# A transformer block's forward and backward: one DMA transpose of the attention backward is held back until the next block's double transpose and issued directly ahead of it

## The chip, the core and the metric

The kernel runs as one program on one core of a Trainium2 chip. The core has five engines that this document names as the profile does: PE (TensorE, matrix products and transposes into PSUM), DVE (VectorE), ACT (ScalarE), POOL (GpSimd) and SP (SyncE). SP computes nothing here: its instruction queue issues nearly all DMA transfers, one after the other. The metric is the device time of one execution in microseconds (us), compared as the median over several executions.

## The reference, cut to what matters

The program returns the output of a parallel block and the gradients of its input and of five weight matrices. `x` is 2048 tokens by 448 features, there are 16 heads of 28 features, and the feed-forward part has 1792 hidden units.

```
xn  = layernorm(x)
qkv = xn @ wqkv                               # 16 heads, Dh = 28
p   = softmax(q @ k.T * Dh**-0.5)             # per head, 2048 x 2048
out = x + (p @ v) @ wo + (silu(xn @ w_gate) * (xn @ w_up)) @ w_down
_, vjp = jax.vjp(f, x, wqkv, wo, w_gate, w_up, w_down)
grads  = vjp(grad_out)                        # six gradients
```

What the change touches is the attention backward: per head, `ds = p * (dO @ v.T - delta)` is formed tile by tile, and the gradient of the queries is `dq = ds @ k * scale`. Here `ds` has query rows on the partitions, and the product for `dq` needs it with key rows on the partitions, so every `ds` tile is transposed once. The gradients of `k` and `v` take `ds` and `p` as they are.

## The kernel before, in words

**Forward, to about 617 us.** The projections, the attention forward, the feed-forward part and its weight gradients are interleaved by hand. Queries, keys and what the backward needs of them (tensors `QD_d` and `KD_d`) are written to device memory.

**Backward, from about 617 us.** A list `steps` of 512 steps runs over 4 groups of heads (`g`), 2 pairs of heads in each (`hp`), 4 key chunks of 512 (`kc`), 4 query chunks (`qc`) and 4 query tiles of 128 (`qi`). Four steps with the same `qc` make a **block**; there are 128 blocks, numbered `b` from 0. One step treats one query tile against 512 keys for two heads (`j` = 0, 1). The main loop (L1235) goes through `k`, and iteration `k` does, in program order:

- `row(k)` (L802): two score products into PSUM tiles `sb` for step `k` (L810), and two products into PSUM tiles `db` for step `k-1` (L818).
- `ew(k)` (L833): two exponentials on ACT for step `k` (tile `e_sb`, L837) and two multiplications on DVE for step `k-1`, which write the tile `ds_sb` (L845). One `ds_sb` tile holds two query tiles: `qi` 0 and 1, or `qi` 2 and 3. There are five such buffers. After the multiplications of `qi` 1 and of `qi` 2 it calls `dst_dma`.
- stores that have come due (`flush`, L797, issued from L800) and loads that are spread over the steps (`drop`, L755, issued from L767); all go to the SP queue. The loads fill query and key tiles (`qd`, `kd`), and the operands of other products that are slipped in between the steps (`h_c`, `x_c`, `o_c`, `dau_c`, `wguT`, `dc`).
- `kv` (L907): four products for the gradients of keys and values (L918, L922).
- once per block, `tr_unit(b)` at `k = 4b + 8`: the `ds` tile of `qi` 3 is transposed on PE (L900) and copied to `dsT` by ACT (L905). In the last block `qi` 2 goes this way as well.
- once per block, `dq_unit(b)` at `k = 4b + 13`: 16 products (L949) of the block's `dsT`, then one addition into `dq_acc`.
- pieces of other products in the time that is left (`fill_step`).

**The transposes by DMA.** `dst_dma(b, ds, qi)` (L824) is called twice per block. At `qi` 1 it takes a new `dsT` buffer (three of them) and issues one DMA transpose of two query tiles from SP; this document calls it the **double** (L830, 128 times). At `qi` 2 it issues one of one query tile, the **third** (L826, 127 times, since the last block has none). With block `b` the double is issued in iteration `4b + 2`, the third in `4b + 3`.

**Who waits for them.** `dq_unit(b)` on PE needs both. The DVE multiplication that takes the same `ds_sb` buffer again, five tiles later, needs the transpose to have read it: for the double that is in iteration `4b + 11` (block `b + 2`, `qi` 2), for the third in `4b + 13` (block `b + 3`, `qi` 0).

**What sets the order.** Every engine runs its instructions in program order and waits by semaphores where data or buffers are missing. SP is such an engine: a transfer stands behind all that were given to SP before it, whether its own data are there or not. Each DMA of SP also waits for the one eight places earlier, since eight semaphores are used in turn.

Of the kernel before, what the change touches and what calls it, by code (L numbers as in the profile page):

```python
# [103 lines left out]
def kernel(  # L104
# [23 lines left out]
    PE, DVE, ACTE, POOL, SP = nc.tensor, nc.vector, nc.scalar, nc.gpsimd, nc.sync  # L128
# [418 lines left out]
    for i in range(len(chain) + LEAD):  # L547
# [4 lines left out]
        k = i - LEAD  # L552
        if k >= 0:
            b = chain[k]
# [98 lines left out]
    for t in range(4):  # L653
        run(T_unit(xnT, xn_t, t, t % 2 == 0, ps_s if t < 2 else None))
    DVE.tensor_reduce(out=r_ones[:],
                      in_=ident_f[:].rearrange("p (a b) -> p a b", b=HP)[:, :, 28:30],
# [11 lines left out]
    for c in range(3):  # L668
        k = 4 * c
# [116 lines left out]
    dqT, dkv, acc, dsT = {}, {}, {}, {}  # L786
# [34 lines left out]

    bk, pend = None, []

    def dst_dma(b, ds, qi):  # L824
        if qi == 2:
            SP.dma_start_transpose(out=dsT[b][:, 2].rearrange("p j kt s -> p (j kt) s"),  # L826
                                   in_=ds[:, 0].rearrange("p j k -> p (j k)"))
            return
        dsT[b] = bk.tile([P, 4, 2, 4, P], BF16, name="dsT", bufs=3)
        SP.dma_start_transpose(out=dsT[b][:, 0:2].rearrange("p q j kt s -> p (q j kt) s"),  # L830
                               in_=ds[:].rearrange("p q j k -> p (q j k)"))

    def ew(k):  # L833
        if k < NB:
            est[k] = kq.tile([P, 2, 512], BF16, name="e_sb", bufs=5)
            for j in range(2):
                ACTE.activation(out=est[k][:, j], in_=sps.pop((k, j))[:], func=ACT.Exp, scale=SCALE)  # L837
        if 1 <= k <= NB:
            g, hp, kc, qc, qi = steps[k - 1]
            b = (k - 1) // 4  # L840
            if qi % 2 == 0:
                dss[k - 1] = dss[k] = kq.tile([P, 2, 2, 512], BF16, name="ds_sb", bufs=5)
            ds = dss[k - 1]
            for j in range(2):
                DVE.tensor_tensor(out=ds[:, qi % 2, j], in0=dps.pop((k - 1, j))[:], in1=est[k - 1][:, j], op=ALU.mult)  # L845
            if qi == 1 or qi == 2 and b < NB // 4 - 1:
                if bk is None:
                    pend.append(lambda: dst_dma(b, ds, qi))
                else:
                    dst_dma(b, ds, qi)  # L850
# [9 lines left out]
    k = n = 0  # L860
# [374 lines left out]
    for k in range(NB + 12):  # L1235
# [21 lines left out]
        if m == 0:  # L1257
            b = (k - 8) // 4
# [6 lines left out]
        elif m == 1:  # L1265
            b = (k - 13) // 4
# [122 lines left out]
```

The softmax here doesn't subtract the row's maximum and nothing guards it: scores larger than these inputs give would overflow.

## Time and profile before

| What | Value |
|---|---|
| median of 13 runs | 1467.3 us (1464.23 to 1475.64) |
| the profiled execution, its time | 1468.93 us |
| the profiled execution, its span | 1467.1 us |
| granted TensorE clock, mean | 0.977 |
| PE, DVE, ACT busy | 92%, 79%, 86% of the span |
| queue of the transfers that SP issues (q1) | 86.9% of 16 DMA engines' span |
| doubles, L830 | 128, median 3067 ns on the SP queue |
| thirds, L826 | 127, median 1256 ns on the SP queue |

The profile is one execution, recorded by the hardware. Its span is the time from the first instruction to the last. A page of it lists groups of instructions by line; in a row like `L845 DVE TENSOR_TENSOR ds_sb<-db,e_sb ... x1024 | 648.6, 685 | 68.8 <-PE db L818 21.8` the line is followed by the engine, the operation, the tile written and the tiles read, the number of instructions, the busy time and the mean of one in ns, and then the engine's idle time directly before these instructions with what ended most of it. `SPq` rows are DMA instructions on the SP queue; their duration is how long the queue was held by the issue, and the data land later. A list of waits names who waited for whom, with the sum, the number of times and the longest. A timeline gives rows in order of time: start, duration, engine, line, operation, tiles, count, and in brackets the idle time before.

### The profile page before, as it was taken

To read this page: it belongs to the slowest core of one execution; us is meant where nothing else is said; L and a number is where in the kernel's file an instruction comes from. 1 tells how busy PE (TensorE), PEld (TensorE's weight loads), DVE (VectorE), ACT (ScalarE), POOL (GpSimd) and SP (SyncE) were. 2 spreads that over 40 slices of the span, in tenths; PEclk is the share of its full clock that TensorE was granted. 3 is DMA by queue.
4 is the path that set the end of the run, shared out by engine and by line. 5 is a ranking of instruction groups with operands and counts; after the bars stand their busy time and mean duration, and the time that the engine had idled before them with its cause. 6 is when DMAs were issued, how large, how long until landed. Compare 5 with 4: busy or idle time off the path is not lost. (4 is left out here: it accounts for less than half of the span.)

```text
span 1467.1 us, 34402 instructions
## 1 busy us (share of the span) xinstructions
PE 1345.0 (92%) x12708; PEld 543.4 (37%) x12708; DVE 1154.5 (79%) x1997; ACT 1262.6 (86%) x2193; POOL 362.6 (25%) x486
## 2 busy tenths in 40 slices
PE   5899999989999999898999989999899999899996
PEld 2333333333333333332333334433343444343343
DVE  6577756756667667487898879888889999899988
ACT  5798989988999988687798979899889999888974
POOL 6465514553344444010001101001001011010005
PEclk9899999999999999998999999999999999999998
DMA  5797957696678675799999999999999999999971
GB/s 151 160 205 184 219 116 187 156 198 163 156 173 186 141 183 132 207 191 198 215 202 202 214 207 188 204 200 209 218 198 189 206 211 214 214 190 196 206 143 59
DMA packets 697664, 271.14 MB, mean 185 GB/s; under 512 B 616128, under 2 KB 672152, under 8 KB 697496
## 3 DMA queue, kind: packets, MB, share of 16 engines
q1 hardware_dynamic: 692520, 262.82, 86.9%
q0 software_dynamic: 3568, 5.83, 1.9%
q8 instruction: 100, 1.64, 0.5%
q14 instruction: 68, 0.56, 0.1%
q10 hardware_dynamic: 1408, 0.30, 0.1%
HBM read 65.04 MB, written 59.90 MB: 85 GB/s over the span
## 5 line engine op out<-in xcount | busy, mean ns | idle before, releaser
L845 DVE TENSOR_TENSOR ds_sb<-db,e_sb 128x512 bf16<-128x512 f32 x1024 | 648.6, 685 | 68.8 <-PE db L818 21.8
L837 ACT ACTIVATE e_sb<-sb 128x512 bf16<-128x512 f32 x1024 | 554.8, 611 | 63.2 <-PE db L818 47.0
L611 ACT ACTIVATE eT<-s_w 128x1024 bf16<-128x1024 f32 x256 | 263.5, 1029 | 46.9 <-PE s_ps L608 44.0
L613 ACT ACTIVATE eT<-s_ps 128x512 bf16<-128x512 f32 x512 | 280.4, 612 | 0.0
L818 PE MATMUL db<-kd,qd 32*128 32x512 bf16 x1024 | 239.3, 386 | 17.2 <-DVE ds_sb L845 16.4
L810 PE MATMUL sb<-kd,qd 32*128 32x512 bf16 x1024 | 211.9, 390 | 8.1 <-DMA qd<-QD_d 4.6
L964 POOL TENSOR_TENSOR dq_acc<-dq_acc,dq_st 128x256 f32<-128x256 f32 x64 | 46.4, 725 | 587.2 <-ACT dq_st L962 587.2
L922 PE MATMUL acc<-ds_sb,qd 128*32 128x512 bf16 x1024 | 162.0, 393 | 0.0
L918 PE MATMUL acc<-e_sb,qd 128*32 128x512 bf16 x1024 | 160.1, 393 | 1.4 <-DVE dw_o L527 1.4
L905 ACT COPY dsT<-db 128x1024 bf16<-128x1024 bf16 x128 | 130.1, 1016 | 31.4 <-PE db L900 30.8
L379 POOL TENSOR_TENSOR nn<-nn,ag 128x512 f32<-128x512 f32 x56 | 71.2, 1271 | 250.9 <-DVE ag L377 242.3
L608 PE MATMUL s_ps<-QQ,KK 32*128 32x512 bf16 x512 | 126.0, 386 | 4.0
L1132 PE MATMUL genb<-wguT,dau_c 128*128 128x448 bf16 x448 | 117.8, 355 | 6.6 <-ACT dq_st L962 3.8
L608 PE MATMUL s_w<-QQ,KK 32*128 32x512 bf16 x512 | 100.4, 387 | 11.7 <-ACT eT L611 10.2
L810 PEld LDWEIGHTS <-qd 32*128 32x128 bf16 x1024 | 48.3, 91 | 153.8 <-issue 141.4
L420 PE MATMUL gen<-xn_t,f_sp 128*128 128x448 bf16 x416 | 91.8, 354 | 2.6 <-DVE nn L394 1.7
L949 PE MATMUL genb<-dsT,kd 128*32 128x256 bf16 x2048 | 80.6, 278 | 5.8 <-DVE y L1084 3.9
L420 PEld LDWEIGHTS <-f_sp 128*128 128x128 bf16 x640 | 55.7, 98 | 75.9 <-issue 31.9
L900 PE MATMUL db<-ident_bf,ds_sb 128*128 128x128 bf16 x1032 | 80.9, 223 | 1.1 <-DVE ds_sb L845 1.1
L900 PEld LDWEIGHTS <-ds_sb 128*128 128x128 bf16 x1032 | 69.6, 100 | 27.5 <-issue 8.7
L380 POOL TENSOR_TENSOR nn<-nn,tt 128x512 f32<-128x512 f32 x56 | 72.0, 1286 | 4.4
L450 PE MATMUL gen<-eT,VS 128*32 128x512 bf16 x1024 | 68.9, 386 | 3.1 <-DVE hda L407 1.1
(163 smaller groups left out, 1882.5 us busy)
## 6 DMA issues: line engine op xcount, KB each, us to landing
F_d<-hda SPq DMA_DIRECT2D x56, 384.0 KB
dau_c<-F_d SPq DMA_DIRECT2D x56, 256.0 KB
h_c<-F_d SPq DMA_DIRECT2D x24, 256.0 KB
qd<-QD_d SPq DMA_DIRECT2D x24, 256.0 KB
dc<-dqkvT_d SPq DMA_DIRECT2D x12, 384.0 KB
dsT<-ds_sb SPq DMA_TRANSPOSE x255
wT_d<-wT_f SPq DMA_DIRECT2D x14, 256.0 KB
KD_d<-qk_sp SPq DMA_DIRECT2D x7, 512.0 KB
```

The costliest lines, as they stand in the source:

```text
L420: PE.matmul(ps[:, :D], lhsT=fsp[fc][:, t // 4, w, t % 4, :], rhs=rhs[:, t, :], start=(t == 0), stop=(t == NT - 1))
L608: PE.matmul(sp4[hh], lhsT=KK[g][r:r + HP, kt * P:(kt + 1) * P], rhs=QQ[g][r:r + HP, qsl], start=True, stop=True, tile_position=(r, 0))
L611: ACTE.activation(out=e2[0][:], in_=wide[:], func=ACT.Exp, scale=SCALE)
L613: ACTE.activation(out=e2[1][:, j], in_=sp4[2 + j], func=ACT.Exp, scale=SCALE)
L810: PE.matmul(s_ps[:], lhsT=qside[g, qc][r:r + HP, 0, qi * P:(qi + 1) * P], rhs=kside[g, kc][r:r + HP, 0, :], start=True, stop=True, tile_po ...
L818: PE.matmul(d_ps[:], lhsT=qside[g, qc][r:r + HP, 1, qi * P:(qi + 1) * P], rhs=kside[g, kc][r:r + HP, 1, :], start=True, stop=True, tile_po ...
L837: ACTE.activation(out=est[k][:, j], in_=sps.pop((k, j))[:], func=ACT.Exp, scale=SCALE)
L845: DVE.tensor_tensor(out=ds[:, qi % 2, j], in0=dps.pop((k - 1, j))[:], in1=est[k - 1][:, j], op=ALU.mult)
L900: PE.transpose(ps[:, c, :], ds[:, qi % 2, c // 4, (c % 4) * P:(c % 4 + 1) * P], ident_bf[:])
L905: ACTE.copy(out=o, in_=ps[:])
L918: PE.matmul(a[r:r + HP, :], lhsT=sp4[:, 1, r:r + HP], rhs=e[:, j, :], start=first, stop=last, tile_position=(0, r), skip_group_check=True)
L922: PE.matmul(a[r:r + HP, :], lhsT=sp4[:, 0, r:r + HP], rhs=ds[:, qi % 2, j, :], start=first, stop=last, tile_position=(0, r), skip_group_ch ...
```

## The change

At `qi` 2 `dst_dma` no longer issues the third; it puts a function that will do so into a list. At the next call with `qi` 1, that is three steps later in the following block, the list is worked off first, and then the double of that block is issued. The third of block `b` so moves from iteration `4b + 3` to `4b + 6`, behind all stores and loads that SP was given in between, and stands directly ahead of the double of block `b + 1`. Number, size, source and destination of all transfers stay; the third still waits for the two DVE multiplications of `qi` 2 and for nothing later. In the SP queue 102 of the 127 thirds change places with one or more other transfers, 200 in all; for the other 25 nothing stood in between and the order stays. The instructions of PE, DVE, ACT and POOL and their order stay too.

```
+    third = []
+
     def dst_dma(b, ds, qi):
         if qi == 2:
-            SP.dma_start_transpose(out=dsT[b][:, 2].rearrange("p j kt s -> p (j kt) s"),
-                                   in_=ds[:, 0].rearrange("p j k -> p (j k)"))
+            third.append(lambda: SP.dma_start_transpose(out=dsT[b][:, 2].rearrange("p j kt s -> p (j kt) s"),
+                                                        in_=ds[:, 0].rearrange("p j k -> p (j k)")))
             return
+        for x in third:
+            x()
+        third.clear()
         dsT[b] = bk.tile([P, 4, 2, 4, P], BF16, name="dsT", bufs=3)
         SP.dma_start_transpose(out=dsT[b][:, 0:2].rearrange("p q j kt s -> p (q j kt) s"),
                                in_=ds[:].rearrange("p q j k -> p (q j k)"))
```

## The prediction

> **What bounds the kernel now.** I read the page's slices first, then stretches of the backward, then the list of waits, then the SP queue's own timeline. The slices: in the right half, which is the backward, the DMA row stands at 9 throughout.
>
> ```profile
> PE   5899999989999999898999989999899999899996
> DVE  6577756756667667487898879888889999899988
> DMA  5797957696678675799999999999999999999971
> ```
>
> The change touches only blocks of that half, so I took four stretches of it (columns: stretch, length, busy us and instruction count of PE, weight loads, DVE, ACT, POOL, then clock, DMA share, GB/s):
>
> ```profile
> 640.00:720.00 80.00, 70.94 (x774) 28.79 (x773) 64.87 (x107) 66.67 (x124) 6.52 (x9) 0.94 1.03 195
> 840.00:870.00 30.00, 22.84 (x241) 9.55 (x237) 21.89 (x37) 20.83 (x40) 0.72 (x1) 0.94 1.07 210
> 1144.00:1204.00 60.00, 58.36 (x681) 23.64 (x681) 57.11 (x94) 56.72 (x107) 4.35 (x6) 1.00 1.09 206
> 1384.00:1412.00 28.00, 27.46 (x322) 11.04 (x319) 26.63 (x45) 26.53 (x50) 3.90 (x6) 1.00 0.83 160
> ```
>
> The last two are bound by compute: PE 97 and 98% busy. In the first two no engine is (76 to 89%), while the DMA share is above 1. Something there waits for transfers, and the waits name it:
>
> ```profile
> PE db L818 <- DVE ds_sb L845: 16.4, 32, 2.2
> DVE ds_sb L845 <- DMA dsT<-ds_sb: 12.5, 10, 2.1
> ```
>
> DVE waits for `ds_sb` buffers that a transpose has not yet read, and PE then for DVE. One such place, SP queue and DVE side by side:
>
> ```profile
> 1034.26 4.11 SPq L830 DMA_TRANSPOSE dsT<-ds_sb  x1
> 1038.41 0.58 SPq L767 DMA_DIRECT2D dau_c<-F_d  x1
> 1039.09 1.23 SPq L826 DMA_TRANSPOSE dsT<-ds_sb  x1
> 1040.37 1.05 SPq L767 DMA_DIRECT2D dau_c<-F_d  x2
> 1041.52 3.40 SPq L830 DMA_TRANSPOSE dsT<-ds_sb  x1
> 1044.97 0.58 SPq L767 DMA_DIRECT2D qd<-QD_d  x1
> ...
> 1048.47 2.48 DVE L845 TENSOR_TENSOR ds_sb<-db,e_sb 128x512 bf16<-128x512 f32 x4 [1.47 <-DMA dsT<-ds_sb]
> ```
>
> The queue has no pause beyond 0.1 us: it is behind. The double issued at 1041.52 is block 64's; its data were ready at 1034.30 (end of the block's fourth L845), so it starts 7.2 us late, lands at 1048.35 (the semaphore updates by which transfers report, in the trace), and DVE starts 0.12 us after that. Over all blocks the double starts more than 2 us after its data in 87 of 128, at most 10.7 us (block 35). Taking every writer that starts within 0.3 us of the landing it needs, the late landings cost DVE 19.9 us: 18.0 for doubles, 1.84 for one third (block 6). They come in five runs: blocks 1 to 13, 14 to 20, 21 to 35, 56 to 67, 93 to 99, 54 blocks in all. There the DMA stream sets the time; elsewhere compute does and the queue has room:
>
> ```profile
> 1388.72 2.69 SPq L830 DMA_TRANSPOSE dsT<-ds_sb  x1
> 1391.50 1.26 SPq L826 DMA_TRANSPOSE dsT<-ds_sb  x1
> 1394.38 1.74 SPq L830 DMA_TRANSPOSE dsT<-ds_sb  x1
> 1396.21 1.88 SPq L826 DMA_TRANSPOSE dsT<-ds_sb  x1
> ```
>
> **The change, part by part.** No instruction comes or goes. In 25 of 127 places nothing stands between third and next double: zero. In the other 102 the third goes behind 1.59 other transfers on the mean (all 127 counted). POOL's queue is not passed.
>
> *1. The copies that the third passes come earlier*, by one third's issue, 1.25 to 1.33 us. What waits for such copies in the whole program: PE for `qd` 4.6 us (2 waits) and `kd` 1.7 us (1 wait). At best three times 1.3; some belong to the start, before any third. Bounds -3.9 and 0; I take -0.5, near zero, since most loads have many steps in hand.
>
> *2. The third lands later.* It waited for nothing behind it on its queue; now it waits until the queue has passed the copies, and only the double stands behind it. A double queued right behind a third lands 2.5 us after it (median of the 18 places where the stream was busy). So in a busy run the third lands 2.5 us before the next double. Its deadline (`ds_sb` of block b+3, `qi` 0, and L949 in the same iteration) is two steps before that double's, 2.9 to 3.3 us at 5.7 to 6.6 us per block. It is thus 0.4 to 0.8 us later against its deadline than the double is. Counted block by block, 19 thirds miss by up to 2.0 us, 18.9 us in sum; counted instead by start plus the third's usual 3.65 us, 6 miss, 4.4 us. But each such miss stands two steps ahead of a place where DVE waits for the next double anyhow, and what is waited at the first is no longer waited at the second. Walking through the blocks with the later of both landings leaves +0.3 us. If PE loses what it can't make up while it stands at L949 with its fillers behind it: up to a third of 18.9, +6. Bounds 0 and +6; I take +0.3, the walk's value.
>
> *3. The stream's own pace.* This decides, since the 54 blocks hang on it: the walk of step 2 with the stream 0.1 us faster per both-sided block (half of it where copies stand on one side only) gives -6 us, 0.1 slower +7, 0.2 slower +14, 0.3 faster -14, and never better than the 19.9. The order of today, double, copies, third, copies, becomes double, all copies, third. Two readings of the same queue disagree.
> Against the change: in the 111 blocks in which the queue never pauses, the time from double to double is 4.41 us without copies (7 blocks), 6.15 with 2.11 copies all behind the third (46), 6.82 with 3.12 copies on both sides (52). The first copies cost (6.15-4.41)/2.11 = 0.82 each, the ones on the other side only (6.82-6.15)/1.01 = 0.66. Grouped at 0.82 a both-sided block would take 6.98, 0.16 more; 36 of the 54 are both-sided: +5.8 us (the walk, which carries the lag on into other blocks, would make it +11).
> For it: a double issued right behind a third holds the queue 2.58 us (mean, 13 places), one right behind a copy 3.20 (97). Over 54 blocks that would be far more than the 19.9 that can be had. But the 13 lie mostly where the stream is not behind (1396.21 above: behind a short double the third takes 1.88 instead of 1.26, and the pair 3.6 against 4.3), so the issue only waits less for data ahead of it. I take the smaller +5.8, from blocks that are behind but with the other row against it, and keep -19.9 and +9.7 (0.27 per both-sided block, by landings instead of issues) as ends.
>
> *Rule against trace.* The DVE wait of 1.47 us above shows a transpose that came too late although SP issued it as early as its place allowed. The Trainium skill, "DMA: Bandwidth & Descriptors", section "Rules for kernel authors", advises to issue a DMA early, compute, and wait for it late. By that rule alone holding the third back would cost its lateness, the 18.9 us of step 2; the trace says that nearly all of it is waited for already, which is the +0.3 in the sum.
>
> **Sum.** Profiled execution 1468.93 = span 1467.1 + 1.8 around it. -0.5 +0.3 +5.8 = +5.6: 1474.5 against that execution. It lies 1.6 above the median of the 13 runs, so against 1467.3 the forecast is 1472.9.
>
> **Rivals.** (a) *Faster: the pair runs better than third and double apart.* Place: every changed block of the five runs. Speaks for it: 2.58 against 3.20 above. Against it: 6.82 against 6.15 shows no extra cost of a third among copies. If a quarter of the 0.62 is real, 0.15 per block, it gives -8: 1459; at 0.3, -14: 1453; all DMA waits gone, 1447.4. It decides from about 0.06 us per changed block, which outweighs step 2. (b) *Nothing: the stream moves the same bytes at the same pace*, and the thirds' lateness hides behind the doubles'. For it: DMA share above 1 in either stretch. -0.5 +0.3: 1467.1. (c) *The third becomes the wait.* PE stands at L949, fillers with it, and the double's wait does not give it back: +6 on top of (b), 1473; with the slower pace too, 1479. Its price stands against it: the third's slack before L949 is 2 us or more in all but ten blocks today, and (c) needs that gone in most of the 54. (d) *The change does nothing because SP runs ahead and waits for data anyway.* True in the 18 blocks whose double starts within 0.3 us of its data, false in the runs, where the queue pauses nowhere.
>
> **How the numbers follow.** Slower, forecast with (c): 0.52, centre 1472.9, its own range 1469.5 to 1483. Faster (a): 0.32. Nothing (b, d): 0.16. About 0.2% (2.9 us) is what this measurement can tell from no change of 1467.3, so 1464.4 to 1470.2 counts as same. The range leaves 1 in 10 on either side: below, the faster case beyond 0.25 us per block, 1455; above, the slower pace by landings plus PE's loss, 9.7 + 6 = 15.7, and a little: 1484.
>
> **What would show it.** Right: the same counts, L826's and L830's doubles adjacent; the DVE wait for the DMA of `dsT` at least as large, now partly at `qi` 0; PE waits at L949 for the DMA appear; the busy stretches 640 to 720 and 840 to 870 take longer. Step 1 wrong: waits for `qd` unchanged. Step 3 wrong: time from double to double shorter at the same copies, doubles held 2 to 2.6 us instead of 3.1, and the wait for `dsT` below 12.5 us. What would make the forecast wrong most easily is the sign of step 3, where the two rows disagree.

## The result and the profile after

The change is faster. Its median is 1461.54 us over 11 runs (1455.96 to 1466.01), that of the kernel before, run beside it, 1470.05 over 48 runs. The ratio is 0.9939 with a 95% interval of [0.9925, 0.9953], some 9 us. The prediction said 1472.9 and slower; the time lies on the other side of no change, near the size of its rival (a). That it lies inside the stated range says little, since 1455 to 1484 took in both signs.

The profiled execution of the change took 1466.01 us (span 1464.2), the slowest of its runs. Two more profiles of it (e7 and e12 below) took 1458.66 and 1458.88, so its sums below are given three times, and those of the kernel before twice (1468.93, and 1469.93 in e8). The granted clock does not tell the two apart: 0.977 and 0.977 before, 0.976, 0.975 and 0.978 after. In the change's code the lines behind L822 stand 5 lower: the third is L828, the double L835, the DVE multiplication L850, the product that takes `dsT` L954.

The page's slices look as before, the DMA row at 9 through nearly all of the backward:

```profile
PE   5899999989999999898898989999999999999996
DVE  6677656756667767487898979888889999999988
DMA  5797857696678685799999999999999999989961
```

The four stretches (columns as before: stretch, length, PE, weight loads, DVE, ACT, POOL, clock, DMA share, GB/s):

```profile
640.00:720.00 80.00, 72.72 (x806) 29.13 (x794) 66.05 (x108) 68.25 (x128) 6.08 (x9) 0.91 1.03 197
840.00:870.00 30.00, 24.57 (x257) 9.03 (x250) 21.90 (x37) 21.45 (x40) 0.73 (x1) 0.94 1.02 210
1144.00:1204.00 60.00, 58.59 (x680) 23.67 (x681) 57.28 (x94) 56.73 (x107) 4.36 (x6) 1.00 1.06 209
1384.00:1412.00 28.00, 27.46 (x309) 10.80 (x301) 26.63 (x44) 26.39 (x50) 3.89 (x6) 1.00 0.81 149
```

The two that compute bounds are as they were. In the two that transfers bound, PE does more in the same time: 72.72 us against 70.94, and 24.57 against 22.84, at the same or a lower clock. The list of waits (who waits, for whom, sum, times, longest) says which waits went and which came:

```profile
DVE ds_sb L850 <- DMA dsT<-ds_sb: 15.6, 14, 2.3
PE genb L954 <- DMA dsT<-ds_sb: 7.0, 8, 1.8
PE db L818 <- DVE ds_sb L850: 5.5, 23, 0.7
PE sb L810 <- DMA qd<-QD_d: 3.7, 1, 3.7
PE sb L810 <- DMA kd<-KD_d: 0.7, 1, 0.7
```

The kernel before has, beside the two lines that the prediction shows:

```profile
PE sb L810 <- DMA qd<-QD_d: 4.6, 2, 3.2
PE sb L810 <- DMA kd<-KD_d: 1.7, 1, 1.7
PE genb L949 <- DMA dsT<-ds_sb: 0.2, 1, 0.2
```

The longest `qd` wait in either list (3.2 and 3.7 us) stands ahead of the first double, where the change does nothing. DVE's wait for the transposes is not smaller in these lists (12.5 and, in e8, 15.2 before; 15.6, 11.5 and 12.7 in the three of the change). But it is another wait: by the prediction's rule (a writer that starts within 0.3 us of the landing it needs) late doubles cost DVE 18.1 and 21.2 us in the two profiles before and 3.3, 1.3 and 3.0 in the three after, late thirds 1.8 and 0.9 before and 14.7, 12.0 and 13.2 after. PE, the busiest engine, waits less for what follows from it: for DVE at `db` 16.4 before and 5.5 now, at L954 for the DMA 0.2 before and 7.0 now, together 16.6 and 12.5.

The same place as in the prediction, block 64, with the queue and, below, DVE:

```profile
1037.66 1.61 SPq L828 DMA_TRANSPOSE dsT<-ds_sb  x1
1039.37 3.62 SPq L835 DMA_TRANSPOSE dsT<-ds_sb  x1
1043.04 0.57 SPq L767 DMA_DIRECT2D qd<-QD_d  x1
1043.70 0.38 SPq L800 DMA_DIRECT2D dqkvT_d<-dkv  x1
1044.13 0.42 SPq L767 DMA_DIRECT2D qd<-QD_d  x1
1044.61 0.51 SPq L767 DMA_DIRECT2D kd<-KD_d  x1
1045.22 1.46 SPq L828 DMA_TRANSPOSE dsT<-ds_sb  x1
1046.77 4.75 SPq L835 DMA_TRANSPOSE dsT<-ds_sb  x1
...
1051.12 1.29 DVE L850 TENSOR_TENSOR ds_sb<-db,e_sb 128x512 bf16<-128x512 f32 x2 [1.39 <-DMA dsT<-ds_sb]
```

The order is double, copies, third, double. Block 64's double starts at 1039.37, 5.35 us behind its data (1034.02), where it was 7.2 before, and lands at 1044.62, two microseconds before its writer wants the buffer. Its third starts at 1045.22 only, lands at 1051.00, and DVE waits 1.39 us for it. Where the queue has room, nothing changed but the pairing:

```profile
1387.88 1.81 SPq L828 DMA_TRANSPOSE dsT<-ds_sb  x1
1391.64 1.74 SPq L835 DMA_TRANSPOSE dsT<-ds_sb  x1
1393.47 1.87 SPq L828 DMA_TRANSPOSE dsT<-ds_sb  x1
```

Where the time went: from the first multiplication of the backward's first step to that of its last, the kernel before takes 801.1 and 800.9 us, the change 797.5, 795.8 and 790.5, on the mean 6.4 less. What lies ahead of it differs between executions of either kernel (614.3 to 619.1 us), and the tail behind it takes 46.8 to 48.2, so one pair of profiles can't give the 9 us of the medians; the blocks hold most of it. The doubles' lag (start after data ready, mean over the five runs' 54 blocks) is 6.26 and 6.23 us before and 5.23, 4.47 and 4.74 after.

### The profile page after: what moved, and what is told of

It is laid out like the page before. It is cut to its first block, busy times and chain, and to the rows that moved or that the text cites. A ratio compares the mean times of both kernels' runs of the same rounds, so it can differ in the third digit from the quotient of the medians.

```text
span 1464.2 us, 34394 instructions
## 1 busy us (share of the span) xinstructions
PE 1346.9 (92%) x12708; PEld 542.9 (37%) x12708; DVE 1153.9 (79%) x1997; ACT 1263.0 (86%) x2193; POOL 362.9 (25%) x486
## 5 line engine op out<-in xcount | busy, mean ns | idle before, releaser
L850 DVE TENSOR_TENSOR ds_sb<-db,e_sb 128x512 bf16<-128x512 f32 x1024 | 648.1, 685 | 64.8 <-PE db L818 21.9
L608 PE MATMUL s_w<-QQ,KK 32*128 32x512 bf16 x512 | 100.1, 386 | 11.7 <-ACT eT L611 10.1
L810 PEld LDWEIGHTS <-qd 32*128 32x128 bf16 x1024 | 48.2, 91 | 151.4 <-issue 141.4
L954 PE MATMUL genb<-dsT,kd 128*32 128x256 bf16 x2048 | 80.8, 279 | 13.8 <-DMA dsT<-ds_sb 7.0
L954 PEld LDWEIGHTS <-kd 128*32 128x32 bf16 x2048 | 54.9, 98 | 51.1 <-issue 19.3
```

The costliest lines, as they stand in the source:

```text
L608: PE.matmul(sp4[hh], lhsT=KK[g][r:r + HP, kt * P:(kt + 1) * P], rhs=QQ[g][r:r + HP, qsl], start=True, stop=True, tile_position=(r, 0))
L810: PE.matmul(s_ps[:], lhsT=qside[g, qc][r:r + HP, 0, qi * P:(qi + 1) * P], rhs=kside[g, kc][r:r + HP, 0, :], start=True, stop=True, tile_po ...
L954: PE.matmul(ps[r:r + HP, :256], lhsT=ks[:, kt, h:h + HP], rhs=t[:, par::2, j, kt, :], start=(kt == 0), stop=(kt == 3), tile_position=(0, r ...
```

## The experiments

Four theories are named in the expectations.

- **A:** what costs is each turn of the queue from copies to a transpose. Fewer turns, faster: 165 before, 113 in the change.
- **B:** what counts is how many copies stand ahead of the third instead of behind it, 200 more in the change; the thirds' lateness is the price.
- **C:** what costs is a third directly behind its own double with nothing between: 64 places before, 14 in the change.
- **F:** what gains is a third directly ahead of the next double: 25 places before, 127 in the change.

One table holds the runs of the whole kernel. The first number is how many more copies pass a third than before, "T-D" the places where a third stands directly ahead of a double, then DVE's waits for late doubles and late thirds, PE's waits that follow from both (`db` for DVE, plus the `dq` product for the DMA), PE's waits for `kd` and `qd` in the blocks, and the length of the blocks, all in us from the profile; then the ratio of times.

| kernel | copies past | T-D | late doubles | late thirds | PE for both | PE for kd, qd | blocks | ratio |
|---|---|---|---|---|---|---|---|---|
| before | 0 | 25 | 18.1, 21.2 | 1.8, 0.9 | 16.6, 16.6 | 3.0, 3.4 | 801.1, 800.9 | 1 |
| the change | 200 | 127 | 3.3, 1.3, 3.0 | 14.7, 12.0, 13.2 | 12.5, 10.7, 10.9 | 0.7, 0, 0 | 797.5, 795.8, 790.5 | 0.9939, 0.9941 |
| e2 | -77 | 15 | 21.5 | 0 | 18.6 | 3.4 | 810.8 | 1.0030 |
| e3, e11 | 145 | 73 | 7.1, 6.9 | 9.2, 6.0 | 12.0, 10.0 | 1.4, 1.3 | 791.5, 791.1 | 0.9917, 0.9931 |
| e4 | 99 | 43 | 7.5 | 6.1 | 12.5 | 1.4 | 796.5 | 0.9954 |
| e5 | 50 | 35 | 21.5 | 1.8 | 19.7 | 2.2 | 802.4 | 1.0011 |
| e9 | 98 | 25 | 6.0 | 7.8 | 10.1 | 1.4 | 797.0 | 0.9958 |
| e10 | 196 | 126 | 3.7 | 14.3 | 10.7 | 0 | 792.4 | 0.9949 |

**e1 and e6: the stream alone.** Only the transfers, without data dependences on any engine: doubles (512 KB), thirds (256 KB) and copies of 256 KB, in the orders named. e1 has three copies per block and also pairs without copies and copies alone; e6 has two copies and more repeats; its loop is shown.

```
+    D2, T1, C = double, third, copy
+    for rep in range(5):
+        run((D2, T1, C, C), 16)
+        run((D2, C, T1, C), 16)
+        run((D2, C, C, T1), 16)
```

> This kernel leaves the whole computation out: it only issues DMAs from SP, in stretches of 30 blocks that differ in order alone, each stretch twice. A block is one double (128x2048), one third (128x1024) and three copies of 256 KB. Stretch 1: double, copy, third, copy, copy. Stretch 2: double, third, three copies. Stretch 3: double, three copies, third (so the third stands in front of the next double). Stretch 4: double and third alone. Stretch 5: three copies alone. Theory A (a changeover from copies to transposes costs DMA time; the change removes one in 52 of 127 blocks): stretches 2 and 3 take 0.15 to 0.4 us less per block than stretch 1. Theory B (the order of bytes is nothing to the stream, the gain comes from copies that land earlier or from something in the compute): the three take the same within 0.05 us. The prediction's own reading: stretch 1 is 0.16 us shorter than 2 and 3.

Measured, us per block, two repeats: double, copy, third, two copies 6.60 and 6.57; double, third, three copies 6.75 and 6.62; double, three copies, third (the change's order) 6.65 and 6.60. Double and third without copies 3.83 and 3.84, three copies alone 2.05 and 2.03. The orders differ by less than the repeats do: neither A's gain of 0.15 to 0.4 us nor the 0.16 us that the prediction feared shows with three copies.

> Again DMAs alone, no computation: blocks of one double, one third and two copies of 256 KB in three orders, 16 blocks each, the three orders in turn five times. Theory C: double, third, copy, copy takes 0.05 to 0.15 us longer per block than double, copy, third, copy and double, copy, copy, third. Theory B: the three agree within 0.03 us.

Measured over five repeats (standard deviation over them): third directly behind the double 5.926 +- 0.060, third between the copies 5.616 +- 0.022, third behind both copies 5.802 +- 0.029 us per block. The SP queue's timeline of the three orders (start, duration, line, tiles):

```profile
601.30 3.32 SPq L147 DMA_TRANSPOSE dT<-ds_sb  x1
604.66 1.30 SPq L151 DMA_TRANSPOSE tT<-ds_sb  x1
606.01 1.07 SPq L142 DMA_DIRECT2D cp<-HB  x2
607.12 3.44 SPq L147 DMA_TRANSPOSE dT<-ds_sb  x1
...
701.50 2.96 SPq L147 DMA_TRANSPOSE dT<-ds_sb  x1
704.50 0.57 SPq L142 DMA_DIRECT2D cp<-HB  x1
705.12 1.24 SPq L151 DMA_TRANSPOSE tT<-ds_sb  x1
706.40 0.58 SPq L142 DMA_DIRECT2D cp<-HB  x1
707.03 3.37 SPq L147 DMA_TRANSPOSE dT<-ds_sb  x1
...
803.95 3.52 SPq L147 DMA_TRANSPOSE dT<-ds_sb  x1
807.52 1.05 SPq L142 DMA_DIRECT2D cp<-HB  x2
808.62 1.24 SPq L151 DMA_TRANSPOSE tT<-ds_sb  x1
809.90 3.33 SPq L147 DMA_TRANSPOSE dT<-ds_sb  x1
```

The order matters at equal bytes. Against the kernel before, whose blocks have the first order (50 blocks) and the second (52), the third order gains 0.12 us on the first and loses 0.19 on the second. So the stream alone does not say that the change gains; the second half is even what the prediction feared. Theory B's forecast for this stream, agreement within 0.03 us, fails here. Landings differ too: a double lands 5.47 us after its start when two copies stand directly ahead of it, 4.98 behind a third and 4.85 behind third and one copy; a third lands after 3.15 us directly behind a double, 3.81 behind one copy, 4.33 behind two. In this stream a transpose that stands behind copies lands later after its start. In the kernel the thirds show it: over the blocks whose double starts more than 1.5 us late they land 3.74 and 3.72 us after their start before and 4.39, 4.44 and 4.39 with the change. The doubles hardly do (5.53 and 5.48 before, 5.40 in all three after); what they gain is above all their earlier start.

**e2: the opposite order, same turns as the change.** The third stays, the copies due between double and third wait until behind the third, so that double, third and copies follow each other.

```
-            flush(k)
-            if 2 <= k:
-                drop()
+            if k % 4 != 2 or k == NB:
+                flush(k)
+                for _ in range(2 if k % 4 == 3 else 1):
+                    if 2 <= k:
+                        drop()
```

> The third stays where it was, and the transfers that stood between a double and its third wait until the third is issued. Changes from a copy to a transpose on the SP queue: 113 as with the change (before: 165); no copy comes earlier, 77 come later. Theory A (time goes with the number of changes from copies to transposes, 8.5 us for 52 of them): ratio 0.993 to 0.995, that is -7 to -10 us, or a little better, since no third is late. Theory B (copies that land earlier make the gain, 8.5 us for 200 copies that pass a third): 77 copies in the other direction, +3 us, ratio 1.002.

Measured: ratio 1.0030 [1.0011, 1.0049], 4.4 us slower. The queue turns from copies to a transpose 113 times, as in the change, and gains nothing from it: theory A falls. Its list of waits:

```profile
PE db L818 <- DVE ds_sb L845: 18.6, 36, 2.0
DVE ds_sb L845 <- DMA dsT<-ds_sb: 12.2, 12, 2.3
```

No third is late here, all of DVE's wait is for doubles, and PE's wait at `db` is 2.2 us above before.

**e3, e4 and e11: the third held back less.** e4 issues it at `qi` 3 of its own block, e3 at `qi` 0 of the next, in either case ahead of that iteration's copies. Of the change, the list `third` stays, and where it is worked off moves:

```
-        for x in third:
-            x()
-        third.clear()
         dsT[b] = bk.tile([P, 4, 2, 4, P], BF16, name="dsT", bufs=3)
...
+            if qi == 0:        # e4: qi == 3
+                for x in third:
+                    x()
+                third.clear()
             if qi == 1 or qi == 2 and b < NB // 4 - 1:
```

> The third is held back by two steps instead of three: it is issued at qi 0 of the next block, ahead of that iteration's copies. 145 copies pass it (with the change 200), and there are 167 changes from copies to transposes (before: 165, with the change 113). Theory A: 0 us, ratio 0.999 to 1.001. Theory B: -6 us, ratio 0.996.

> The third is held back by one step: issued at qi 3 of its own block. 99 copies pass it, and it stands between copies more often: 194 changes from copies to transposes (before: 165). Theory A: 29 changes more at 0.16 us, +5 us, ratio 1.003. Theory B: -4 us, ratio 0.997.

Measured: e3 0.9917 [0.9891, 0.9943], 1456.96 us; e4 0.9954 [0.9929, 0.9980], 1461.28 us. A expected no gain and a loss; both gain, as B has it, though e3 gains twice what B said (0.996) and its interval leaves B's value out. e3 was run once more:

> e3 again, on the same chip as the two others: third issued at the next block's first query tile, 145 copies pass it. Theory B with the thirds' lateness as a price: 0.990 to 0.994 as in e3, at or a little below the change's 0.994, since the thirds come later by fewer copies. Theory F: 73 thirds directly ahead of a double against 127 in the change, so less gain than the change, 0.996.

Measured: 0.9931 [0.9905, 0.9957], 1459.90 us. In both batches e3 is the fastest of the versions measured in it; the change was in neither, and its interval overlaps that of e3. The waits of e3's first run:

```profile
DVE ds_sb L847 <- DMA dsT<-ds_sb: 11.9, 12, 2.4
PE db L818 <- DVE ds_sb L847: 9.0, 30, 1.0
PE genb L955 <- DMA dsT<-ds_sb: 3.0, 4, 1.9
```

DVE's lateness is shared between doubles and thirds (7.1 and 9.2 us in the table), and PE waits at the `dq` product 3.0 us instead of 7.0.

**e5: exactly one copy between.** The third is issued as soon as one other transfer has followed the double. It takes apart 50 of the 64 places where third and double touch, and does little else. Of its edit, the part that decides:

```
+    def sp_copy(o, i):
+        SP.dma_start(out=o, in_=i)
+        since[0] = True
+        for x in third:
+            x()
+        third.clear()
```

> The third is issued as soon as one other transfer has gone out behind its double, and not later: where one had already gone out it stays where it was before, else it waits for the first one, at most until the next double. 50 copies pass a third (with the change 200); a third directly behind its double is left in 14 of 127 blocks (before 64, with the change 14, in the run with the pair kept together 126). Theory C (what costs is the third directly behind its double): the whole gain of the change and a little more, since the third is hardly late: -8 to -12 us, ratio 0.992 to 0.9945. Theory B (the gain goes with the number of copies that pass a third): 50 of 200, -2 us, ratio 0.9985.

Measured: 1.0011 [0.9992, 1.0029]. Theory C falls. B's -2 us lies a little outside the interval (-1.2 to +4.3), and the 0.31 us per block that e6 gives for this very edit is not there at all: the stream alone and the stream in the kernel differ.

```profile
PE db L827 <- DVE ds_sb L860: 19.5, 34, 1.9
DVE ds_sb L860 <- DMA dsT<-ds_sb: 16.7, 11, 2.3
```

The doubles stay as late as before.

**e9: many copies ahead of the third, and still one behind it.** This separates B from F. The last load that is due is kept back until the third has gone:

```
         while slow and credit > 0:
-            _, _, o, i = slow.pop(0)
-            SP.dma_start(out=o, in_=i)
-            credit -= size(o)
+            put()                          # issues what was kept
+            kept.append(slow.pop(0))
+            credit -= size(kept[0][2])
...
         third.clear()
+        put()
         dsT[b] = bk.tile([P, 4, 2, 4, P], BF16, name="dsT", bufs=3)
```

> As the change, but the last copy that is due before a double is kept back and issued behind the third, so that a copy and not the third stands directly ahead of the double: double, copies, third, one copy, double. 98 copies pass a third compared with the kernel before (200 in the change, 99 in e4), but a third stands directly ahead of a double in 25 places only, as in the kernel before (127 in the change, 43 in e4). Theory B (what counts is how many copies go ahead of the third instead of behind it, some 0.07 us of cycle for each one in the blocks that are behind): as e4, -4 to -9 us against the kernel before, ratio 0.994 to 0.997, and the doubles land 5.2 to 5.3 us after their start as e4 has it. Theory F (what counts is that a third stands directly ahead of the double): no change, ratio 0.998 to 1.002, doubles at 5.5.

Measured: 0.9958 [0.9935, 0.9982], 1463.49 us, and doubles land 5.25 us after their start (5.53 and 5.48 before, 5.28 in e4; means over those that start more than 1.5 us after their data). F expected nothing. The interval lies below 1 and only touches F's lower end (0.998); with e3, which gains more than the change with 73 such places against 127, F falls as the main cause. e9 and e4 pass as many copies (98 and 99) by different edits and gain the same.

```profile
DVE ds_sb L860 <- DMA dsT<-ds_sb: 10.5, 13, 2.5
PE db L827 <- DVE ds_sb L860: 7.4, 28, 0.7
PE genb L964 <- DMA dsT<-ds_sb: 2.7, 4, 1.0
```

**e10: the copies moved instead of the third.** The kernel before, with its third in place; the copies of four iterations are issued together behind the double.

```
-            flush(k)
-            if 2 <= k:
-                drop()
+            if m == 2 or k == NB:
+                for now in range(k, k + 4):
+                    flush(now)
+                    drop()
+                now = k
```

> The third stays where the kernel before has it; instead the copies of four iterations are issued together, directly behind the double and so ahead of the third. The SP queue's order is nearly that of the change (double, copies, third, double; 196 copies pass the third) and no third is held back by the program. If the order in the queue is what gains, as B and F both have it: as the change, -6 to -12 us, ratio 0.992 to 0.996. If the gain came from something else in the change (the third's issue being tied to the next double's data): no change or, since copies that are issued early stand ahead of thirds that are ready, slower, 1.000 to 1.004.

Measured: 0.9949 [0.9928, 0.9971], 1461.27 us. The queue's order alone, reached without holding any third back, gives the gain, and the thirds are as late as in the change, since in a queue that is behind the order decides and not the place in the program:

```profile
DVE ds_sb L845 <- DMA dsT<-ds_sb: 14.7, 13, 2.3
PE db L818 <- DVE ds_sb L845: 5.7, 23, 0.7
PE genb L949 <- DMA dsT<-ds_sb: 5.0, 6, 1.5
```

**e7, e8 and e12: both kernels again**, without an edit.

> The changed kernel once more, for a second profile and on the same chip as the one with a copy between. All theories: ratio 0.993 to 0.995. Theory C: 2 to 4 us behind the run with one copy between, the thirds' lateness. Theory B: 6 us ahead of it.

> The kernel before once more, for a second profile: DVE waits for the DMA of dsT near 12 us, its thirds hardly ever the last to land. If its doubles' delays differ much from those of the first profile, differences of a few us between single profiles mean nothing.

> The change once more, for a third profile of it. In the medians the change is 9 to 10 us ahead, but in its two profiles the backward's blocks (first to last block start) take only 3.5 and 5.2 us less than before (801.6), while the part ahead of them differs by up to 5 us between executions of any kernel. If the whole gain lies in the blocks, as theory B has it, the two profiles were slow ones and a third shows 790 to 796 us there; if part of it lies outside, it shows 796 to 799 again.

Measured: the change 0.9941 [0.9916, 0.9965], 1458.74 us; before, one execution, 1469.93 us; the change in its third profile 1458.88 us with 790.5 us for the blocks. All three of the change's profiles have late thirds instead of late doubles; e12 lands in the span that theory B gave for the blocks (790 to 796), the two others at 797.5 and 795.8. The blocks hold most of the gain, and one profile is good to some 3 to 4 us.

**The order's price per block.** The twelve profiles of whole kernels give the time from one double's start to the next for all blocks but block 0 in which both doubles are more than 1 us late (the queue pauses less than 0.5 us in each), sorted by the number of copies and where the third stands (mean, standard error, number of blocks):

| copies | all behind the third | on both sides | all ahead of it |
|---|---|---|---|
| 1 | 5.48 +- 0.08 (39) | | 5.36 +- 0.06 (85) |
| 2 | 6.22 +- 0.07 (77) | 6.14 +- 0.04 (134) | 6.05 +- 0.05 (142) |
| 3 | 6.76 +- 0.08 (47) | 6.70 +- 0.05 (134) | 6.64 +- 0.05 (103) |
| 4 | 7.44 +- 0.18 (10) | 7.27 +- 0.07 (53) | 7.19 +- 0.12 (38) |
| 5 | 7.86 +- 0.31 (7) | 7.90 +- 0.08 (40) | 7.78 +- 0.14 (25) |

In every row the order of the change is the shortest, by 0.2 to 2 standard errors of the difference, so no row shows it alone. By landings the single rows scatter more (6.20, 6.01, 5.76 with two copies, but 6.84, 7.00, 6.88 with three); with the block's identity, the number of copies and the instruction packets in it taken out by least squares, each copy ahead of the third shortens the block by 0.071 +- 0.020 us (994 blocks); by starts the same fit gives 0.041 +- 0.012. Weighted by the rows, a block with all copies behind the third gains some 0.15 us when they go ahead of it, and a both-sided one some 0.08. The 54 blocks of the five runs are 18 of the first kind and 36 of the second. The prediction's own walk through the blocks, with these two values in place of its assumed pace, gives -8.2 (landings) to -8.6 us (starts). It is worked out after the fact and partly from the runs it explains, and it leaves out PE's waits for `kd` and `qd`, some 3 us. With the price per copy in place of the rows' values the walk gives -6 us (starts) to -10 (landings). So the size fits to a few us, and how much of the gain is pace and how much loads that come earlier is not told apart.

**What stays open.** The runs show that the order in the queue is the cause of the gain. The gain does not simply follow the number of copies that go ahead of the third: none at 50, by the ratios 6 to 7 us at 98 and 99, 10 to 12 at 145, 7 to 9 at 196 and 200. The fall at the end fits the thirds' lateness as a price, but that is argued. They don't show why the kernel ranks the orders all behind, both sides, all ahead, while the stream alone has the middle one fastest; e5, which stakes most on that difference, got nothing. Nor is the thirds' lateness priced by itself: no run has the change's order with thirds that are on time. More `ds_sb` buffers would give that, and no run has them.

## Why the prediction was wrong, point by point

**What bounds the kernel: right.** The stream bounds the 54 blocks. All the gain that can be placed lies in the waits behind transposes and loads, and an order of the queue that adds and removes no byte changes the time by 0.3% up or 0.8% down. (The 76 to 89% quoted for the two busy stretches are PE's; DVE and ACT stand at 69 to 83%.)

**Step 1, copies earlier: sign right, size wrong.** Taken at -0.5 us out of -3.9 to 0. In the blocks PE waits 3.0 and 3.4 us for `kd` and `qd` before and 0.7, 0 and 0 after, some -3. The step argued that most loads have many steps in hand; the few that had none were the whole sum, and each of them was helped: one `qd` wait of 1.3 us is gone, the `kd` wait of 1.7 falls to 0.7 and, in two of three profiles, to nothing. (The mean of 1.59 transfers passed per third should read 1.57, 200 over 127.)

**Step 2, thirds later: right in its mechanism; its +0.3 us was not measured by itself.** It counted 19 thirds that miss by 18.9 us in sum and said that these waits take the place of the doubles'. Measured: 16, 12 and 13 places with 14.7, 12.0 and 13.2 us, the waits for doubles down to 3.3, 1.3 and 3.0, and waits at the `dq` product, 7.0, 6.2 and 5.5 us. This is rival (c)'s mechanism, which the prediction held unlikely, and yet not its cost: PE's waits at `db` fall by 11 to 12 us at the same time.

**Step 3, the stream's pace: the step that failed, by its sign.** The forecast hung on +5.8 us, a stream that slows by 0.16 us per both-sided block; the runs show it faster, by some 0.08 us there and 0.15 where all copies stood behind the third. It took this from the reading that "the first copies cost (6.15-4.41)/2.11 = 0.82 each, the ones on the other side only (6.82-6.15)/1.01 = 0.66". These are blocks with different numbers of copies, and the third copy is cheaper than the first two wherever it stands: the twelve profiles have 4.49 us without copies, then 5.40, 6.12, 6.69, 7.26, steps of 0.91, 0.72, 0.57 and 0.57. At equal numbers the profile before alone had 6.14 (25 blocks, behind) against 6.15 (17, both sides) with two copies, and 6.81 (11) against 6.65 (19) with three. So the row that decided the sign was not in the trace; comparing at equal numbers would have left nothing sure, and the forecast at rival (b) with (a) open. The order's true effect, 0.08 to 0.15 us, could not be had from that trace, since among its blocks whose queue never pauses none with two copies or more has them all ahead of the third.

**The row on the other side** (a double holds the queue 2.58 us behind a third, 3.20 behind a copy) was rightly doubted: the doubles that follow the 54 blocks hold it 3.27 us in both profiles before and 3.20, 3.20 and 3.19 after. It pointed the right way at a tenth of the size.

**Rival (a)** at 0.15 us per block gave -8 and 1459. Measured are 0.08 and 0.15 by kind of block, -9 and 1461.5 (1458.7 in e7). That its size comes out is luck: its reason, that third and double run better as a pair, is theory F, and e9 gains without the pairs. **Rival (d)** holds where the queue has room, as it said. Of the signs named for step 3, a shorter time from double to double at the same number of copies came, by these 0.08 to 0.15 us; the doubles' hold of 2 to 2.6 us did not come, and the wait for `dsT` did not fall reliably below 12.5 (15.6, 11.5, 12.7), because late thirds filled it.

**The rule weighed there** (the Trainium skill, "DMA: Bandwidth & Descriptors", section "Rules for kernel authors": issue a DMA early and wait late) would by itself have cost the thirds' lateness. The trace agrees that the thirds come late, 12.0 to 14.7 us where the forecast had 18.9, and disagrees on the outcome: in a queue that is behind, an earlier third is paid for by the doubles and loads after it. e2, in which the thirds go ahead of 77 copies more, loses 4.4 us.

## What to carry to other kernels

In a stretch that one DMA queue bounds, the order of transfers was worth some per mille here even though every byte stays: try the copies ahead of the transfer that has slack, and measure it in the whole kernel, since the stream alone ranked the orders otherwise. Read the price of an order only from blocks with the same number of transfers; a cost per transfer that falls with their number looks just like an effect of where they stand. A sum of waits that stays can hide a change of who waits: split it by the transfer waited for, and follow it to the engine that bounds.

## What the runs showed that was not expected

- When a transpose lands depends on its neighbours, and not on one of them alone. In the stream alone a double takes 5.47 us from start to landing behind two copies and 4.98 behind a third; in the kernel, over all twelve profiles and the doubles more than 1.5 us late, 5.60 (two copies ahead, a copy and a third behind it; 89 doubles) against 5.13 (third ahead, same behind; 68). But with two copies behind it the two are alike, 5.37 (two copies ahead; 33) and 5.36 (third ahead; 299), and the latter is the order of the change.
- With two copies ahead, a double with a third directly behind it lands later: 5.86 us (130 doubles, third and copy behind) against 5.60 (89, copy and third behind). With a third and one copy ahead there is no such difference: 5.35 (39) and 5.34 (111).
- Transposes run at 768 KB in 3.83 us alone, 205 GB/s; copies at 768 KB in 2.05 us, 384 GB/s; mixed, a block of double, third and three copies takes 6.6 us, 0.7 more than the two sums.
- 100 packets of 16 KB on the instruction queue are moved beside these transfers. By least squares over the late blocks of each profile, a block with such a packet is 0.9 to 1.6 us longer by landings, and a copy adds 0.65 to 0.80.
